# Score tasks issued in pairs during the projections, and a second buffer for the retrieved memory rows, in a fused two-branch attention kernel

## The chip, the cores and the metric

The kernel runs on one core of one Trainium2 chip. A core has a matrix engine (TensorE, PE in the profile; its weight loads are listed apart as PEld), a vector engine (VectorE, DVE), a scalar engine (ScalarE, ACT), a general engine (GpSimd, POOL) and a queue processor (SyncE, SP) that here only issues DMAs. They run side by side, each through its own list of instructions in order, and wait for one another on semaphores. The metric is device time in microseconds (us) of the whole program; lower is better. All inputs and outputs are float32.

## The reference

Two attention branches on the same input of 2048 rows and 512 columns, 32 heads of 16, mixed by a gate per row. Branch A works in four segments of 512 rows: causal softmax attention inside the segment, and beside it a read of a running memory (a 16x16 matrix and a normaliser per head) that earlier segments have filled. Branch B is ordinary full softmax attention.

```python
for s in range(4):                                  # branch A, segment s
    logits = einsum("bhqd,bhkd->bhqk", qs, ks) * scale + mask
    a_dot = einsum("bhqk,bhkd->bhqd", softmax(logits), vs)
    pq = phi(qs)                                    # t + 1 if t > 0 else exp(t)
    num = einsum("bhld,bhde->bhle", pq, M)
    den = einsum("bhld,bhd->bhl", pq, z)[..., None] + 1e-6
    outs.append(g * num / den + (1 - g) * a_dot)
    M = M + einsum("bhld,bhle->bhde", phi(ks), vs)
    z = z + phi(ks).sum(rows)
a = concat(outs) @ wo
b = softmax(qB @ kB.T * scale) @ vB @ wob           # branch B
out = gate * a + (1 - gate) * b
```

## The kernel before

All instructions are issued in the order in which the program writes them; each engine keeps that order.

**Projection stage** (to about 349 us). Queries, keys and values are computed by jobs of 12 matmuls of 128x128 by 128x512 (v_job, L255; qk_job, L274): three products of high and low halves, over four slices of the 512 columns. A job takes one PSUM bank from a pool of six, later four (misc, L95, the bank not used for longest). For a query or key job ScalarE copies the bank into st[:, 0], VectorE subtracts to get the remainder st[:, 1], and SP writes both halves to device memory (two DMAs; st has four buffers). Where branch A needs phi, VectorE takes the minimum with 0 (L285), ScalarE the exponential (L288), VectorE the maximum and sum (L291), all before the bank is free.

The loop of 16 blocks (L722) goes over branch A: block = 4 g + c, for four groups g of eight heads and four segments c. In each block come the query job, the key job, then for c > 0 the memory read: mem_out (L304) multiplies phi(q) by the memory state on TensorE in two halves, ScalarE copies the denominators to recm and the numerators to om, VectorE divides. mem_put (L323), later in the same block, transposes om on TensorE, scales it on ScalarE back into om, and SP writes it out by a DMA (L331). The next memory read, one block later, writes om again; om has one buffer. mem_tr and mem_upd (c < 3) update the memory. Between these parts stand two or three fill jobs of either branch.

**Score tasks for maxima.** The softmax of unit u needs the largest score of each row. s_b (L442) computes a 128x512 block of scores for two heads (two matmuls of 64 rows, in the two halves of the array) into one of two score banks of PSUM (SBK, taken in turn), and VectorE reduces it to maxima (L451, 1.22 us). s_a (L417) does the same with a mask for branch A. A task's matmuls must wait until the reduction of the task before last has freed its bank. From block 4 to block 13 the 38 tasks of units 32 and 0 are spread over the projections: each block adds 3.8 to a quota, and spill (L714), called after each part of a block, issues a task for each whole unit of quota that is there. What is left of them is issued at the end of block 13. In blocks 14 and 15 six tasks of unit 33 follow in the same way, on keys that load_kb(1, ...) brings in.

**From block 14 on** SP's list holds, in order: four DMAs of constant rows (set_aux, L148), load_kb in four parts of four DMAs (L369) with the jobs' and mem_put's writes between them, the writes of block 15's query and key job (L295), and then the four small DMAs of m_rows (L484), which bring the row maxima into the last rows of the query tiles qb and qa. The first score product of the next stage (t_group, L503, tile tb<-qb,kb) reads those rows.

**Score stage** (349 us to the end): 32 rounds, each with one unit of each branch: scores, exponentials on ScalarE, products with the values, and the maxima tasks of the next unit. The last four fill jobs stand in the first round.

Of the kernel before, what the change touches and what calls it, by code (L numbers as in the profile page):

```python
# [7 lines left out]
FT = mybir.dt.float32  # L8
# [10 lines left out]
E = 16  # L19
# [14 lines left out]
def gated_mix_kernel(ctx, tc, x, wq, wk, wv, wo, beta, wqkv, wob, gate_w, out):  # L34
# [36 lines left out]
    X = proj.enter_context(tc.tile_pool(name="proj", bufs=1))  # L71
# [23 lines left out]
    def misc():  # L95
        return bank(mode["misc"])
# [204 lines left out]
    def mem_state(g, c):  # L301
        return MST[c % 2][g % 2]

    def mem_out(g, c):  # L304
        m = mem_state(g, c)[:, :, :E + 1]
        o = X.tile([128, 4, 8, E], FT, name="om")
        r = X.tile([128, 4, 8], FT, name="recm")
        for n in range(2):
            b = misc()[:, :16 * (E + 1)].rearrange("p (i h e) -> p i h e", i=2, h=8)
            for i in range(2):  # L310
                nc.tensor.matmul(b[:, i], PHI[g, 0, c][:, (2 * n + i) * 128:(2 * n + i + 1) * 128], m,
                                 start=True, stop=True)
            nc.scalar.activation(r[:, 2 * n:2 * n + 2], b[:, :, :, E], AF.Copy)
            nc.scalar.activation(o[:, 2 * n:2 * n + 2].rearrange("p i h e -> p (i h) e"),
                                 b[:, :, :, :E].rearrange("p i h e -> p (i h) e"), AF.Copy)
        nc.vector.tensor_scalar(r, r, 1e-6, None, op0=OP.add)
        nc.vector.reciprocal(r, r)
        nc.vector.tensor_tensor(r, r, gate[:, 4 * c:4 * c + 4, None].to_broadcast([128, 4, 8]), op=OP.mult)
        o3 = o.rearrange("p i h e -> p (i h) e")
        nc.vector.tensor_tensor(o3, o3, r.rearrange("p i h -> p (i h)")[:, :, None].to_broadcast([128, 32, E]), op=OP.mult)  # L320
        PHI[g, "o", c] = o
# [258 lines left out]
    def o_cols(c, t):  # L580
        return AT["o"][c % 2][:, :, :, t * 128:(t + 1) * 128]
# [57 lines left out]
    def s_tasks(u):  # L639
        return [todo(s_a, u, *t) for t in ST_A] if u < 32 else [todo(s_b, u, *t) for t in ST_B]  # L640
# [60 lines left out]
    first = s_tasks(32) + s_tasks(0)  # L701
    st33 = [todo(s_b, 33, *t) for t in sorted(ST_B, key=lambda t: t[2])]
    early = st33[:EARLY]
# [8 lines left out]
    quota = 0  # L712

    def spill():  # L714
        nonlocal quota
        if quota >= 1:
            quota -= 1
            (first or early).pop(0)()

    S0 = [b[:, 0] for b in SBK]  # L720
    CUM = (2, 4, 6, 9, 11, 13, 16, 18, 20, 22, 24, 27, 29, 32, 34, 36)
    for blk in range(16):  # L722
# [14 lines left out]
        if c == 3 and g < 3:  # L737
            split_w(0, "A", g + 1, (0,))
        spill()
        if blk == 0:  # L740
            split_wv(3)
            do_beta()
        if blk > 0:
            if pc == 0:
                mem_upd(pg, pc)
        qk_job(0, "A", g, 1, c)
        spill()
        if c == 2 and g < 3:
            load_w("A", g + 1)
# [18 lines left out]
        if c > 0:  # L768
            mt[0] += [todo(mem_out, g, c)]
            mt[2] += [todo(mem_put, g, c)]  # L770
        if c < NC4 - 1:
            mt[1 + (c == 0)] += [todo(mem_tr, g, c)]
        for n in range(3):
            for f in mt[n]:
                f()
            if blk == 14 and n == 2:
                quota = EARLY
            if mt[n]:
                spill()
            if blk == 14:  # L780
                load_kb(1, 1 + n)
            if nf == 35:
                mode["misc"] = [MB, PVB, TB[1]]
            if nf < want:
                fill[nf]()
                spill()
                if nf in (18, 24):
                    load_w("B", 2 + nf // 24)
                if nf in (15, 20, 26):
                    split_w(2 if nf == 20 else 1, "B", nf // 5 - 2)  # L790
                nf += 1
        if blk == 13:
            for f in first:
                f()
            first, quota = [], 0
# [160 lines left out]
    for t in range(4):  # L956
        d = den[:, t * 128:(t + 1) * 128]
        o = o_cols(3, t)[:, 3, 0]
# [36 lines left out]
```

## Time and profile before

| | us |
|---|---|
| median of the runs | 1983.9 |
| lowest, highest of 3 runs | 1976.98, 1985.88 |
| profiled execution, first to last instruction (span) | 1976.0 |
| TensorE busy in the span | 1944.8 |
| VectorE busy | 1630.3 |
| ScalarE busy | 1435.7 |
| GpSimd busy | 257.5 |

The profile records one execution. The span leaves out what lies before the first and after the last instruction; the fastest run lies 0.98 us above it. In the timelines, a row is a run of like instructions on one engine: its start in us from the span's start, its length in us, engine, line of the program, operation, output tile <- input tiles, shapes, and the count. A number in square brackets is the engine's idle time before the row, with what ended it. Lengths of matmuls overlap a little (they are pipelined), so the cost of a piece of work is read from the start of one row to the start of the next. "SPq" rows are DMAs being issued by SP.

### The profile page before, as it was taken

The page shows a single profiled execution, that of the slowest core. Times are in us where ns is not written, and L with a number is a line of the kernel's source. Part 1 is how long each engine was busy: PE and PEld are TensorE (multiplying, and loading weights), DVE is VectorE, ACT ScalarE, POOL GpSimd, SP SyncE. Part 2 cuts the span into 40 slices and gives each one's busy share as a digit, 9 for nine tenths or more (in the row PEclk, how much of TensorE's full clock was granted, in tenths as well). Part 3 has the DMA queues.
Part 4 walks back from the last instruction along what each step waited for, and adds up shares of the span by engine and source line. Part 5 has one row for each costly group of instructions (what it writes and reads, how often), then busy time and mean ns, then how long its engine had stood idle before and what let it go on. Part 6 is the DMA issues. An engine that isn't in the chain of part 4 may idle for free.

```text
span 1976.0 us, 43643 instructions
## 1 busy us (share of the span) xinstructions
PE 1944.8 (98%) x17517; PEld 945.6 (48%) x17517; DVE 1630.3 (83%) x1825; ACT 1435.7 (73%) x2703; POOL 257.5 (13%) x474
## 2 busy tenths in 40 slices
PE   8999999999999999999999999999999999999999
PEld 6887777434344344444444444444444444444435
DVE  6135665899999999999999999999999999999942
ACT  3233332688888888888888888888888888888884
POOL 2200000011210101111010101010101010101012
PEclk9999999999999999999999999999999999999999
DMA  6766656644443444344445353444344444444111
GB/s 205 172 209 183 191 186 173 152 111 114 97 114 88 103 86 103 86 114 86 114 85 112 86 113 86 114 86 114 86 108 91 96 102 87 102 90 103 48 51 57
DMA packets 162742, 222.49 MB, mean 113 GB/s; under 512 B 39260, under 2 KB 89452, under 8 KB 156780
## 3 DMA queue, kind: packets, MB, share of 16 engines
q1 hardware_dynamic: 159596, 211.70, 44.0%
q0 software_dynamic: 2944, 8.00, 2.1%
q8 instruction: 138, 2.26, 0.5%
q14 instruction: 64, 0.52, 0.1%
HBM read 148.21 MB, written 68.16 MB: 109 GB/s over the span
## 4 chain that ended last, share of the span: by engine, by line
PE 90%; DMA 3%; DVE 2%; ACT 2%; issue 1%; SPq 1%; ACTq 0%; DVEq 0%
PE pvb L525 31%; PE tb L503 17%; PE sbk L449 12%; PE mb L503 8%; PE tb L279 3%; PE tb L591 2%; PE mb L279 2%; PE sbk L427 2%; PE pvb L279 2%; PE tb L262 2%; DVE mxb L451 1%; ACT raw L509 1%; PE mb L591 1%; PE mb L262 1%; PE sbk L431 1%
## 5 line engine op out<-in xcount | busy, mean ns | idle before, releaser
L451 DVE TENSOR_REDUCE mxb<-sbk 128x2 f32<-128x1024 f32 x1024 | 1226.1, 1222 | 36.6 <-PE sbk L449 32.4
L509 ACT ACTIVATE raw<-tb 128x512 f32<-128x512 f32 x1557 | 888.2, 598 | 163.1 <-PE tb L503 90.7
L525 PE MATMUL pvb<-raw,vb 128*17 128x256 f32 (+1 forms) x8072 | 639.4, 388 | 0.0
L509 ACT ACTIVATE raw<-mb 128x512 f32<-128x512 f32 x780 | 466.4, 598 | 76.5 <-PE tb L503 44.8
L503 PE MATMUL tb<-qb,xh 64*128 64x512 f32 x872 | 330.8, 496 | 1.7 <-ACT raw L509 1.7
L525 PEld LDWEIGHTS pvb<-raw,vb 128*17 128x17 f32 x8072 | 134.4, 95 | 341.7 <-issue 336.6
L449 PE MATMUL sbk<-xh,qb 64*128 64x512 f32 x1344 | 283.1, 398 | 2.0 <-DMA xh<-dB 0.8
L503 PE MATMUL mb<-qb,xh 64*128 64x512 f32 x445 | 219.6, 494 | 0.0
L503 PEld LDWEIGHTS tb<-qb,xh 64*128 64x128 f32 x872 | 124.4, 183 | 188.1 <-issue 91.4
L512 POOL TENSOR_SCALAR_AFFINE_SELECT raw<-raw 128x256 f32<-128x256 f32 (+1 forms) x320 | 116.1, 363 | 700.1 <-ACT raw L509 692.3
L503 PE MATMUL tb<-qb,kb 64*128 64x512 f32 x471 | 176.3, 496 | 1.4 <-DMA qb<-mr 0.8
L435 DVE TENSOR_REDUCE mx<-sbk 128x2 f32<-128x768 f32 (+1 forms) x128 | 139.8, 1092 | 43.1 <-PE sbk L431 37.1
L449 PE MATMUL sbk<-kb,qb 64*128 64x512 f32 x704 | 150.6, 406 | 1.2 <-DVE mxb L451 1.1
L449 PEld LDWEIGHTS sbk<-xh,qb 64*128 64x128 f32 x1344 | 137.9, 186 | 7.3 <-DVE mxb L451 3.5
L503 PEld LDWEIGHTS mb<-qb,xh 64*128 64x128 f32 x445 | 81.3, 183 | 86.6 <-issue 48.0
L503 PE MATMUL mb<-qb,kb 64*128 64x512 f32 x233 | 115.4, 495 | 0.7 <-DVE st L289 0.7
L565 POOL TENSOR_TENSOR o<-o,d 128x512 f32<-128x512 f32 x31 | 39.8, 1283 | 562.6 <-DMA d<-rd 281.6
L503 PEld LDWEIGHTS tb<-qb,kb 64*128 64x128 f32 x471 | 66.0, 183 | 98.4 <-issue 52.5
L525 PE MATMUL pvb<-raw,va 128*17 128x256 f32 (+2 forms) x1280 | 94.7, 383 | 5.8 <-ACT pvs L534 5.8
L427 PE MATMUL sbk<-ka,qa 64*128 64x256 f32 (+3 forms) x512 | 86.8, 346 | 1.2 <-ACT raw L509 1.2
L503 PE MATMUL tb<-qa,ka 64*128 64x384 f32 (+3 forms) x340 | 79.2, 372 | 0.0
L449 PEld LDWEIGHTS sbk<-kb,qb 64*128 64x128 f32 x704 | 71.6, 185 | 12.6 <-issue 6.5
(273 smaller groups left out, 1790.7 us busy)
## 6 DMA issues: line engine op xcount, KB each, us to landing
xh<-dB SPq DMA_DIRECT2D x38, 512.0 KB
vb<-vdB SPq DMA_DIRECT2D x16, 1088.0 KB
dB<-st SPq DMA_DIRECT2D x64, 256.0 KB
dA<-st SPq DMA_DIRECT2D x64, 256.0 KB
pd<-pvs SPq DMA_DIRECT2D x64, 256.0 KB
kb<-dB SPq DMA_DIRECT2D x22, 512.0 KB
xh<-dB SPq DMA_DIRECT2D x38, 256.0 KB
qb<-dB SPq DMA_DIRECT2D x64, 128.0 KB
```

Of the source, the lines that this page charges most:

```text
L262: nc.tensor.matmul(b, lhs, WV[wi][:, k, :], start=n == 0, stop=n == 11)
L279: nc.tensor.matmul(b, WS[ws][w][wi][:, k, :], (XH, XL)[xi][c][:, k, :], start=n == 0, stop=n == 11)
L427: nc.tensor.matmul(b[:, j, c0:c0 + n], q_of(u)[r, p, i * 128:(i + 1) * 128], k_of(u, p)[r, :n], start=True, stop=False)
L435: nc.vector.tensor_reduce(m[:, :, p, i], b[:, :, :n], axis=AX.X, op=OP.max)
L449: nc.tensor.matmul(b[:, j], q_of(u)[r, p, i * 128:(i + 1) * 128], k_of(u, p)[r, kc * C:(kc + 1) * C], start=True, stop=True)
L451: nc.vector.tensor_reduce(MXB[u][:, :, p, i, kc], b, axis=AX.X, op=OP.max)
L503: nc.tensor.matmul(bs[j][:, c0:c0 + w], k_of(u, h // 2)[r, 128 * it:128 * it + 128], q_of(u)[r, h // 2, q0:], start=True, stop=True)
L509: nc.scalar.activation(pt, bs[j], AF.Exp, scale=SCALE)
L512: nc.gpsimd.affine_select(out=m, in_=m, pattern=[[1, 128]] if n < 2 else [[0, 2], [1, 128]], compare_op=OP.is_ge, fill=0.0, base=0, channe ...
L525: nc.tensor.matmul(PVB[32 * h:32 * h + E + 1, q0 + lo:q0 + hi], vt[:, it, 4 * q + h, :], pt[:, lo:hi], start=it == 0 and lo == 0, stop=it ...
L565: nc.gpsimd.tensor_tensor(o, o, d, op=OP.mult)
L591: nc.tensor.matmul(b, (AT["oh"], AT["ol"])[oi][:, g, a], (AT["wh"], AT["wl"])[wi][:, g, a], start=n == 0, stop=n == 11)
```

## The change

spill waits until two units of quota are there and then issues two tasks in a row; the number of tasks does not change. The tile om gets two buffers (recm beside it keeps one).

```diff
     def mem_out(g, c):
         m = mem_state(g, c)[:, :, :E + 1]
-        o = X.tile([128, 4, 8, E], FT, name="om")
+        o = X.tile([128, 4, 8, E], FT, name="om", bufs=2)
         r = X.tile([128, 4, 8], FT, name="recm")
...
     def spill():
         nonlocal quota
-        if quota >= 1:
-            quota -= 1
-            (first or early).pop(0)()
+        if quota >= 2:
+            quota -= 2
+            for _ in range(2):
+                (first or early).pop(0)()
```

With two units at a time the tasks of a block stand behind its query job and its key job (in blocks 4 and 13 behind the query job alone), no longer behind mem_out and the fill jobs; two masked tasks of unit 0, not one, are left for the end of block 13. In block 14 two pairs follow mem_put and mem_upd, in block 15 one pair follows the query job.

## The prediction

> **What bounds the kernel now.** I read the page first, then the busy time by stretch, then TensorE's waits, then the timelines of TensorE, VectorE and the SP queue around the two edits. The page and the stretch from 200 to 310 us (columns: stretch, length, busy PE, PEld, DVE, ACT, POOL, granted clock, DMA share, GB/s):
>
> ```profile
> PE 1944.8 (98%) x17517; PEld 945.6 (48%) x17517; DVE 1630.3 (83%) x1825; ACT 1435.7 (73%) x2703; POOL 257.5 (13%) x474
> ```
>
> ```profile
> 200.00:310.00 110.00, 110.00 (x549) 82.09 (x548) 73.20 (x108) 36.40 (x78) 3.92 (x6) 1.00 0.60 190
> ```
>
> TensorE has no idle time in the heart of the projection stage; VectorE is busy for two thirds of it. So an edit there is worth what it takes off TensorE's queue, or what it makes TensorE wait. TensorE's waits between 140 and 380 us (total, times, longest) are few:
>
> ```profile
> PE tb L279 <- ACT om L314: 3.0, 1, 3.0
> ...
> PE tb L503 <- DMA qb<-mr: 0.8, 1, 0.8
> ...
> PE pvb L262 <- DVE phi L291: 0.7, 1, 0.7
> ```
>
> The first is the memory rows' single buffer, once, at the end of block 15. TensorE there, with ScalarE and SP (start, length; a number in brackets is idle time before):
>
> ```profile
> 316.99 0.62 PE L311 MATMUL tb<-mst,phi 128*128 128x136 f32 x4
> 317.37 2.12 PE L279 MATMUL tb<-xh,wv 128*128 128x512 f32 x8
> ...
> 338.81 0.49 PE L449 MATMUL sbk<-xh,qb 64*128 64x512 f32 x2
> 342.30 3.78 PE L279 MATMUL tb<-xh,wv 128*128 128x512 f32 x8 [3.00 <-ACT om L314]
> ...
> 347.59 0.92 PE L327 MATMUL mb<-ident,om 128*128 128x128 f32 x4
> 349.33 0.50 PE L503 MATMUL tb<-qb,kb 64*128 64x512 f32 x2 [0.83 <-DMA qb<-mr]
> ```
>
> ```profile
> 341.86 0.38 ACT L314 ACTIVATE om<-tb 128x256 f32<-128x256 f32 x1 [6.65 <-DMA om<-om]
> ```
>
> ```profile
> 311.18 6.96 SPq L148 DMA_DIRECT2D xh<-aux  x4
> ...
> 340.24 3.68 SPq L295 DMA_DIRECT2D dA<-st  x4
> ...
> 344.02 2.58 SPq L484 DMA_DIRECT2D qb<-mr  x2
> ```
>
> ```profile
> 345.34 3.95 DMA qb<-mr
> ```
>
> The reader is to see two things. ScalarE's wait stops TensorE for 3.00 us; but the score stage that follows cannot begin before the rows of m_rows have landed (345.34 + 3.95 = 349.29), and SP issues those in its own time: its queue works from 311.18 to 346.60 with hardly a gap, on transfers ordered before them. The chain of waits goes through both.
>
> **The change, part by part.**
>
> *Doubled buffer.* It removes ScalarE's wait at block 15: the buffer then used was last read by the transfer of block 13, two products back. TensorE would start the last job 3.00 us sooner, and would not run it slowly. How slowly is seen from its rows: 342.30 to 347.59 is 5.29 us, where such a job elsewhere takes 2.88 (below), so 2.4 more, and the four transposes take 347.59 to 348.50, about 0.5 more than the usual 0.4. The granted clock says why:
>
> ```profile
> 344.00:346.00 2.00, 2.00 (x6) 1.52 (x6) 2.00 (x3) 0.00 (x0) 0.00 (x0) 0.50 0.53 184
> ...
> 348.00:350.00 2.00, 1.17 (x10) 0.72 (x8) 0.69 (x1) 1.25 (x3) 0.00 (x0) 0.94 0.32 66
> ```
>
> After 3 us of idling the clock is 0.50, and full again near 348.2, some 5.8 us after work resumed. All this (3.0 + 2.4 + 0.5 = 5.9 us) I cost as a gain of **nothing**: the work that hides it is SP's queue. TensorE would be done with block 15 at about 342.5, then wait for the rows until 349.3, which is late next. If that cover were gone, the gain would be the 5.9 us. What remains is worse than nothing: TensorE now idles some 6.8 us, so it is the score stage that begins at half clock, on the path to the end. 5.8 us at half clock lose 2.9 us of work; the first job alone loses 2.4. I take **+2.6 us**; the lower bound is 0 (the clock returns at once), the upper 2.9 if it returns as it did before.
>
> The Trainium skill ("TensorE: Matmul & The Clock Gate", Part 1) has the clock halve after about 3.4 us without work and return after about 3.4 us of it. By that the loss would be about 1.7 us (an estimate from that page) and the sum 0.9 us lower; the trace agrees on the halving, but its slow stretch was longer.
>
> *Two at a time: what TensorE saves.* Timeline of TensorE, first for a score task alone:
>
> ```profile
> 142.34 2.11 PE L262 MATMUL sbk<-wv,xh 128*128 128x512 f32 x8
> ...
> 145.22 2.03 PE L279 MATMUL tb<-xh,ws 128*128 128x512 f32 x8
> ...
> 184.04 0.63 PE L311 MATMUL pvb<-mst,phi 128*128 128x136 f32 x4
> 184.60 0.49 PE L449 MATMUL sbk<-kb,qb 64*128 64x512 f32 x2
> 185.03 2.13 PE L262 MATMUL tb<-wv,xh 128*128 128x512 f32 x8
> ...
> 188.02 0.49 PE L449 MATMUL sbk<-kb,qb 64*128 64x512 f32 x2
> 188.44 0.65 PE L336 MATMUL tb<-ident,phi 128*128 128x128 f32 x4
> ```
>
> A job of 12 matmuls after another takes 145.22 - 142.34 = 2.88 us; with a task it is 188.44 - 185.03 = 3.41, so a task alone costs 0.53. After mem_out it costs more: the half of the memory product before it takes 0.56 (184.04 to 184.60) against 0.38 without (316.99 to 317.37), the task 0.43, the job after it 2.99 against 2.88: 0.72. A second task behind a first shows only in the score stage:
>
> ```profile
> 372.15 0.64 PE L449 MATMUL sbk<-xh,qb 64*128 64x512 f32 x4
> 372.72 0.63 PE L525 MATMUL pvb<-raw,vb 128*17 128x256 f32 x8
> ...
> 375.21 0.40 PE L449 MATMUL sbk<-xh,qb 64*128 64x512 f32 x2
> 375.54 0.63 PE L525 MATMUL pvb<-raw,vb 128*17 128x256 f32 x8
> ```
>
> Two take 0.57, one 0.33: the second costs 0.24. Of the 38 tasks up to block 13, 19 become second ones; following the quota through the loop, 7 of them come from places after mem_out, 12 from others: 7 x 0.72 + 12 x 0.53 - 19 x 0.24 = **6.8 us saved**.
>
> *Two at a time: what it costs.* Each task needs one of two score banks, and a bank is free when VectorE's reduction of it is done. The rows that time it, TensorE's task after the block's first job, then VectorE's reduction of it:
>
> ```profile
> 213.76 0.51 PE L449 MATMUL sbk<-kb,qb 64*128 64x512 f32 x2
> ...
> 227.20 0.51 PE L449 MATMUL sbk<-kb,qb 64*128 64x512 f32 x2
> ...
> 231.54 0.51 PE L449 MATMUL sbk<-kb,qb 64*128 64x512 f32 x2
> ```
>
> ```profile
> 215.11 1.22 DVE L451 TENSOR_REDUCE mxb<-sbk 128x2 f32<-128x1024 f32 x1
> ...
> 229.91 1.22 DVE L451 TENSOR_REDUCE mxb<-sbk 128x2 f32<-128x1024 f32 x1
> ```
>
> ```profile
> 244.50 0.51 PE L449 MATMUL sbk<-kb,qb 64*128 64x512 f32 x2
> ...
> 260.85 0.51 PE L449 MATMUL sbk<-kb,qb 64*128 64x512 f32 x2
> ```
>
> ```profile
> 247.17 1.22 DVE L451 TENSOR_REDUCE mxb<-sbk 128x2 f32<-128x1024 f32 x1
> 248.30 0.68 DVE L285 TENSOR_SCALAR phi<-tb 128x512 f32<-128x512 f32 x1
> ...
> 264.11 1.22 DVE L451 TENSOR_REDUCE mxb<-sbk 128x2 f32<-128x1024 f32 x1
> ```
>
> Count from the start of a block's first pair. VectorE first has that block's first job to finish, then two reductions 1.13 apart (247.17 to 248.30). In blocks 6 and 10 (c = 2) they end at 3.80 and 4.93. TensorE is back with the second pair at 3.65 (0.24 for the second task, 3.41 for the first and the job); its second task starts at 4.93 and ends at 5.36, not 4.32: 1.1 us of waiting, counted as roundly as the hand-over allows. In 7 and 11 (c = 3) a weight split is queued ahead on VectorE, so the reduction starts at 264.11 - 260.85 = 3.26, the banks come free at 4.39 and 5.52: 1.6 us. In 8 and 12 (c = 0) it starts at 1.35 and both banks are free in time: 0. In 5 and 9 (c = 1) mem_upd gives more time (231.54 - 227.20 + 0.24 = 4.58 against 3.84 and 4.97): 0.2. In block 5 the 0.7 us wait on phi in the table above grows too, since VectorE reaches the second job later: about 0.7 more. Sum 2 x 1.1 + 2 x 1.6 + 2 x 0.2 + 0.7 = **6.5 us**. Behind the waiting task on TensorE stand mem_out and the fill job; ScalarE and VectorE wait for them, but neither is short of time there. Bounds for saving and cost together: -6.8 (no wait) to +6.5 (no saving); I take **-0.3**.
>
> In blocks 14 and 15 the pairs change only when TensorE is done, ahead of the wait for SP: nothing. SP's long run starts from the last job of block 13, so it shifts by the same -0.3.
>
> Sum: -0.3 + 0 + 2.6 = **+2.3 us**. The span of 1976.0 would become 1978.3. The span is 7.9 under the median of the three runs (1983.9) and 0.98 under the fastest; from the median the forecast is **1986.2 us**. The score stage does not give it back: TensorE is as full there as here.
>
> **The rivals.** (1) *Both edits pay in full*: no bank waits (-6.8) and the end of block 15 closes up (-5.9): 1971.2. For it: the wait removed is on the chain of waits. Against: SP's order, and the reductions' times. The Trainium skill ("Trainium Kernel Development and Optimization", Best Practices) would have double-buffering pay like this; SP's row speaks against it here. Chance 0.10. (2) *Pairs pay, the buffer does not*: -6.8 + 2.6 = -4.2, 1979.7. For: VectorE is a third idle. Against: the two banks. Chance 0.14. (3) *Slower*: the clock stays at half beyond the first job of the score stage, through all four left-over fill jobs, since small matmuls and waits stand between them. 4 x 2.4 = 9.6 us, and about half of the 10 us of smaller work up to 371 as well: +14.6, less 0.3, 1998.2. It decides from 356 us on: if the clock is still 0.50 there. For: an idle time twice as long as the one above. Against: the recovery at 348. Chance 0.18. (4) *The change does not act* (another single buffer, recm, holds ScalarE instead): 1983.9; the earlier product's scaling is long over by then. Chance 0.04. My forecast has 0.54.
>
> **How the numbers follow.** About 0.5% (9.9 us) is what a measurement of this kernel can tell from no change. Faster: rival 1, 0.10. Slower: rival 3 and a small part of the forecast, 0.20. Within: 0.70. The forecast's own range, from the runs' spread and the bounds, is 1980 to 1991. The range given, 1977 to 1996, reaches over rival 2 and into rival 3, and leaves out rival 1 and the rest of 3.
>
> **What would show it.** Right: TensorE's wait on om gone, its wait on qb<-mr about 6 us, clock 0.50 behind it, waits of a task on mxb of 1 to 2 us in blocks 6, 7, 10, 11. Wrong: the first score group well before 349 us, no waits on mxb, or an end of block 13 that lies more than 3 us from where it was.

## The result and the profile after

| | before | after |
|---|---|---|
| median of 21 runs, us | 1981.2 | 1984.27 |
| lowest, highest, us | 1976.2, 1986.2 | 1979.7, 1988.8 |
| span of the profiled execution, us | 1976.0 | 1980.9 |

The ratio is 1.0019 with an interval of 1.0011 to 1.0027: about 3.8 us slower (2.2 to 5.3 us, taking the ratio times 1981.2). The forecast was +2.3 us, within 0.5% of before, inside the range given. The page after:

```profile
PE 1943.0 (98%) x17517; PEld 948.6 (48%) x17517; DVE 1627.8 (82%) x1825; ACT 1434.4 (72%) x2703; POOL 256.6 (13%) x474
```

TensorE's waits between 140 and 380 us after (total, times, longest; two smaller ones, 0.8 and 0.5, left out):

```profile
PE sbk L449 <- DVE mxb L451: 5.1, 9, 0.8
PE tb L503 <- DMA qb<-mr: 4.7, 1, 4.7
PE sbk L449 <- DMA xh<-dB: 3.3, 1, 3.3
PE pvb L262 <- DVE phi L291: 1.1, 1, 1.1
```

The wait on om is gone from the list. In its place stand the wait for the rows of m_rows (0.8 before, 4.7 now), a longer wait for the first keys of unit 33 (0.8, now 3.3), and waits of score tasks on the reductions of their banks, which before came to 0.4. Busy TensorE is 1.8 us less than before, yet the span is 4.9 longer. The end of block 15 on TensorE's timeline, after:

```profile
347.01 0.60 PE L327 MATMUL mb<-ident,om 128*128 128x128 f32 x4
352.27 0.50 PE L503 MATMUL tb<-qb,kb 64*128 64x512 f32 x2 [4.65 <-DMA qb<-mr]
...
353.36 3.45 PE L279 MATMUL mb<-xh,wv 128*128 128x512 f32 x8
...
357.66 0.50 PE L503 MATMUL tb<-qb,kb 64*128 64x512 f32 x2
```

Block 15 now closes without the stop on om (a wait of 0.48 us behind VectorE, at 341.3 us, is new), and TensorE idles afterwards. The first fill job of the score stage then takes 357.66 - 353.36 = 4.30 us; before, 2.98 (350.22 to 353.20):

```profile
350.22 2.12 PE L279 MATMUL mb<-xh,wv 128*128 128x512 f32 x8
...
353.20 0.50 PE L503 MATMUL tb<-qb,kb 64*128 64x512 f32 x2
```

The granted clock (third number from the end) says why. After:

```profile
354.00:356.00 2.00, 2.00 (x6) 1.60 (x5) 1.40 (x2) 0.00 (x0) 0.00 (x0) 0.50 0.55 198
356.00:358.00 2.00, 2.00 (x11) 1.34 (x9) 0.00 (x0) 0.23 (x1) 0.00 (x0) 0.93 0.79 227
```

Block 7 after shows the other half of the change, on TensorE's timeline:

```profile
195.96 0.74 PE L449 MATMUL sbk<-kb,qb 64*128 64x512 f32 x4
196.62 2.12 PE L279 MATMUL pvb<-xh,ws 128*128 128x512 f32 x8
...
200.50 0.49 PE L449 MATMUL sbk<-kb,qb 64*128 64x512 f32 x2 [0.83 <-DVE mxb L451]
201.63 0.49 PE L449 MATMUL sbk<-kb,qb 64*128 64x512 f32 x2 [0.64 <-DVE mxb L451]
...
203.31 3.38 PE L279 MATMUL mb<-xh,wv 128*128 128x512 f32 x8
...
207.45 2.02 PE L279 MATMUL pvb<-xh,wv 128*128 128x512 f32 x8
...
260.44 0.74 PE L449 MATMUL sbk<-kb,qb 64*128 64x512 f32 x4
...
267.48 3.67 PE L279 MATMUL tb<-xh,wv 128*128 128x512 f32 x8
...
271.91 2.02 PE L279 MATMUL mb<-xh,wv 128*128 128x512 f32 x8
```

The first pair goes through in 0.66 us (195.96 to 196.62), and both tasks of the second wait for a bank. Behind them and the memory product the next job takes 4.14 us (203.31 to 207.45), not 2.88, and in block 11 its counterpart 4.43 (267.48 to 271.91). There the clock has dropped too, in block 7 as shown and in block 11 to 0.50 from 268 to 270 us:

```profile
202.00:204.00 2.00, 2.00 (x12) 1.86 (x11) 2.00 (x3) 0.75 (x4) 0.00 (x0) 0.67 0.79 246
204.00:206.00 2.00, 2.00 (x6) 1.56 (x5) 1.84 (x6) 0.16 (x1) 0.00 (x0) 0.50 0.61 210
```

To see where the time went, I use three marks on TensorE: the start of the first score task of block 4, the start of mem_upd at the end of block 13, and the first score product. The rows of before, then of after:

```profile
148.09 0.50 PE L449 MATMUL sbk<-kb,qb 64*128 64x512 f32 x2
...
309.64 1.19 PE L350 MATMUL tb<-vm,pk 128*128 128x136 f32 x8
```

```profile
145.74 0.74 PE L449 MATMUL sbk<-kb,qb 64*128 64x512 f32 x4
...
310.73 1.19 PE L350 MATMUL tb<-vm,pk 128*128 128x136 f32 x8
```

| stretch, us | before | after | difference |
|---|---|---|---|
| start to first task | 148.09 | 145.74 | -2.35 |
| first task to the end of block 13 | 161.55 | 164.99 | +3.44 |
| end of block 13 to the first score product | 39.69 | 41.54 | +1.85 |
| first score product to the end | 1626.67 | 1628.63 | +1.96 |
| span | 1976.0 | 1980.9 | +4.9 |

The first line is for the most part not the change's doing: 1.7 us of it are there by 116 us, where a job at 34 us ran at half speed in the one execution and not in the other. The other 0.6 us lies around a short wait behind om in block 2 of before; e1, which has one buffer too, does not lose it. Single executions differ by such amounts, so the differences between kernels below are taken from the ratios, and the marks only say where inside an execution time went. The profiled execution of before is also one of its shorter ones: 1976.98 us, 4.2 below the median, where that of after (1982.58) is 1.7 below.

The last line of the table adds up three things, and only the first goes with the change. From the first row of score products to the next one after the fill job it takes 3.87 us before (349.33 to 353.20) and 5.39 after (352.27 to 357.66): 1.5 us for the half clock. Before has a wait of 1.12 us on a score bank at 443.7 us that after does not have; seven of the twelve traces (before, e1, e3, e5, e7, e9, e10) have one of 0.6 to 1.1 us there. And near 1910 us, behind two waits of 0.34 and 1.17 us that both have, the clock drops in after (0.72 from 1910 to 1915 us) and not in before (1.00), which costs 1.5 us. All twelve traces have the waits of 0.34 and 1.17 us; the drop is in seven of them (after, e1 to e5, e8) and not in before, e6, e7, e9 and e10, so neither of the two follows the pairs or the buffer.

### The profile page after: what moved, and what is told of

Same layout as the page of the kernel before. It is cut to its first block, busy times and chain, and to the rows that moved or that the text cites. A ratio compares the mean times of both kernels' runs of the same rounds, so it can differ in the third digit from the quotient of the medians.

```text
span 1980.9 us, 43644 instructions
## 1 busy us (share of the span) xinstructions
PE 1943.0 (98%) x17517; PEld 948.6 (48%) x17517; DVE 1627.8 (82%) x1825; ACT 1434.4 (72%) x2703; POOL 256.6 (13%) x474
## 4 chain that ended last, share of the span: by engine, by line
PE 90%; DVE 3%; ACT 3%; DMA 2%; issue 1%; SPq 1%; ACTq 0%; DVEq 0%
PE pvb L525 31%; PE tb L503 17%; PE sbk L449 12%; PE mb L503 8%; PE tb L279 3%; PE tb L591 2%; PE mb L279 2%; DVE mxb L451 2%; PE sbk L427 2%; PE tb L262 2%; ACT raw L509 1%; PE mb L591 1%; PE pvb L279 1%; PE sbk L431 1%; PE mb L262 1%
```

## The experiments

After the result I held this theory (A): pairs save work on TensorE but lose it again to waits for score banks, and the second buffer gives nothing because SP's list, on which the rows of m_rows stand, decides when the score stage starts. The rival (B): the whole loss is the second buffer's, through the half clock behind the longer idle time.

**One part alone.** e1_pairs_only takes the second buffer out of the changed kernel; e2_om_only puts it into the kernel before.

```diff
-        o = X.tile([128, 4, 8, E], FT, name="om", bufs=2)
+        o = X.tile([128, 4, 8, E], FT, name="om")
```

> The changed kernel with one om buffer again. Theory A (waits for score banks and the SP queue cost the time, the second buffer gives nothing): TensorE comes to the last job of block 15 late, so little or nothing of the 3.0 us wait on om is left; the time is within 1 us of the changed kernel, about +3.8 us against before. Theory B (the second buffer costs it, through the half clock at the start of the score stage): the loss goes with the buffer, 0 us against before.

Measured: ratio to before 1.0015 (1.0001 to 1.0028), against 1.0019 for both parts together: as A said, and B's 0 lies just outside the interval. TensorE's waits in e1:

```profile
PE sbk L449 <- DVE mxb L451: 5.8, 10, 0.8
PE tb L503 <- DMA qb<-mr: 4.2, 1, 4.2
PE tb L279 <- ACT om L314: 1.2, 1, 1.2
```

The om wait is 1.2, not 3.0: counted from the end of block 13 (308.16 us in e1), TensorE comes there 0.7 us later than before, and the transfer that frees the buffer is done 1.2 us earlier. The wait for the rows is still 4.2, and the first fill job behind it takes 5.15 us (348.97 to 354.12). So the slow start of the score stage comes without the second buffer too.

> The kernel before with two om buffers, tasks one at a time. Theory A: the wait on om is gone, TensorE waits some 6 us for the rows of m_rows instead and starts the score stage at half clock; +1 to +2.5 us against before. Theory B: the whole loss, +3.8 us. Theory C (the buffer pays): -3 to -6 us.

Measured: 1.0002 (0.9991 to 1.0014). This rules out B and C, whose +3.8 us and -3 us lie outside; A's smaller loss lies inside the interval, and so does no loss at all. e2's timeline where the score stage starts:

```profile
348.38 0.79 PE L503 MATMUL tb<-qb,kb 64*128 64x512 f32 x2 [5.49 <-DMA qb<-mr]
...
349.95 3.39 PE L279 MATMUL mb<-xh,wv 128*128 128x512 f32 x8
...
354.21 0.50 PE L503 MATMUL tb<-qb,kb 64*128 64x512 f32 x2
```

The saved wait turned up as 5.49 us in front of the score stage, and the first fill job took 4.26 us. By the run times the slowdown comes with the pairs, though the intervals of e1 and e2 overlap.

**Pairs without the bank waits.** e3_pairs_spaced keeps two tasks in a row but lets at least two calls of spill pass after each pair.

```diff
-        if quota >= 2:
+        gap += 1
+        if quota >= 2 and (gap > 2 or not first):
+            gap = 0
             quota -= 2
```

> The changed kernel, but a pair is followed by at least two calls of spill without a task up to block 13, so a block's second pair stands after its first fill job. Theory A: no waits of a task on mxb in blocks 6, 7, 10, 11, no half clock in 7 and 11, the end of block 13 about 6 us earlier counted from the first pair; the rows of m_rows earlier by 3 to 5 us, time 0 to -2 us against before. Rival: the tasks' order does not matter, +3.8 us as the changed kernel.

Measured: 0.9999 (0.9987 to 1.001), as A said and 1.0019 excluded. The marks in e3:

```profile
148.52 0.74 PE L449 MATMUL sbk<-kb,qb 64*128 64x512 f32 x4
...
304.54 1.19 PE L350 MATMUL tb<-vm,pk 128*128 128x136 f32 x8
...
346.92 0.50 PE L503 MATMUL tb<-qb,kb 64*128 64x512 f32 x2 [4.54 <-DMA qb<-mr]
```

Up to the end of block 13 it takes 156.02 us: 5.5 less than before, 9.0 less than the changed kernel. No task waits on mxb in blocks 4 to 13 and no job there runs slowly. But from there to the first score product it takes 42.38 us, 2.7 more than before, and TensorE waits 4.54 us for the rows, after 4.2 us for the first keys of unit 33 in block 14. The saving is lost in front of the score stage.

**The half clock.** e4_warm adds work that nothing uses to the changed kernel, and e8_om_warm the same (18 matmuls) to the kernel of e2.

```diff
+    for _ in range(14):
+        nc.tensor.matmul(PVB, WS[0][0][0][:, 0, :], XL[0][:, 0, :], start=True, stop=True)
     for k in range(32):
```

> The changed kernel with 14 idle matmuls of 128x512 into PVB between block 15 and the score stage, in TensorE's wait for the rows of m_rows (3.4 us of work that nothing uses). Theory A: granted clock 1.0 behind the wait, the first fill job of the score stage 2.98 us instead of 4.3; -1.5 us against the changed kernel, about +2.3 us against before. Rival (the half clock costs nothing there): no difference to the changed kernel, or slower by up to 3.4 us.

Measured: 1.0007 (0.9995 to 1.0019); the expected +2.3 us is 1.0012. The rows of e4:

```profile
347.69 3.47 PE L907 MATMUL pvb<-xl,ws 128*128 128x512 f32 x14
353.56 0.50 PE L503 MATMUL tb<-qb,kb 64*128 64x512 f32 x2 [2.40 <-DMA qb<-mr]
...
354.45 2.13 PE L279 MATMUL mb<-xh,wv 128*128 128x512 f32 x8
...
357.44 0.50 PE L503 MATMUL tb<-qb,kb 64*128 64x512 f32 x2
```

The job takes 2.99 us again, and from the first row of score products to the next it takes 3.88 us, as before, not 5.39. (The whole stretch to the end is 1626.6 us, as before, too; that is chance, since e4 has the drop near 1910 us and lacks the bank wait at 443.7.)

> The kernel before with two om buffers and 18 idle matmuls of 128x512 (4.4 us of work that nothing uses) in TensorE's wait ahead of the score stage. Theory A (the half clock behind the wait is all that the second buffer costs): clock 1.0, first fill job 2.98 us; about 2.4 us less than with the buffer alone, -2 us against before. Rival: no difference to the buffer alone.

Measured: 0.999 (0.9978 to 1.0002), about -2 us. The rows of e8:

```profile
351.35 0.50 PE L503 MATMUL tb<-qb,kb 64*128 64x512 f32 x2
...
355.23 0.50 PE L503 MATMUL tb<-qb,kb 64*128 64x512 f32 x2
```

3.88 us here as well, where e2 has 5.83 (348.38 to 354.21). Each interval overlaps that of the kernel without the idle matmuls, so the gain in time is likely rather than proved; the shorter job is plain in both traces.

**What sets the start of the score stage.** e5 (the changed kernel), e6 (before with two om buffers) and e7 (e3) issue two of the four parts of load_kb behind m_rows:

```diff
-            if blk == 14:
-                load_kb(1, 1 + n)
+            if blk == 14 and n == 0:
+                load_kb(1, 1)
...
             m_rows(0)
+            load_kb(1, 2)
+            load_kb(1, 3)
```

> The changed kernel with the third and fourth part of load_kb(1, ...) issued behind m_rows, not ahead of it. Theory A (SP's list sets the start of the score stage): the rows of m_rows land some 6.6 us earlier, before TensorE is done with block 15; its wait on them is gone, the clock stays at 1.0; -4.7 and -2.0 us, so about -3 us against before. Rival (the transfers, not SP's list, hold the rows back): the wait stays near 4.7 us and the time at +3.8.

Measured: 0.9998 (0.9988 to 1.0008), 4 us better than the changed kernel's ratio, but the expected -3 us against before lies outside. In e5 the wait for the rows has gone; a wait of 0.41 us on a bank is what is left there:

```profile
348.42 0.60 PE L327 MATMUL mb<-ident,om 128*128 128x128 f32 x4
349.14 0.49 PE L503 MATMUL tb<-qb,kb 64*128 64x512 f32 x1
350.04 0.49 PE L503 MATMUL tb<-qb,kb 64*128 64x512 f32 x1 [0.41 <-DVE st L289]
```

From the end of block 13 (310.75) to the first score product it takes 38.39 us, 3.15 less than in the changed kernel; the slow jobs of blocks 7 and 11 are still there, and so are 3.5 us of waiting for the first keys of unit 33.

> The kernel before with two om buffers and the same later load_kb parts, tasks one at a time. Theory A: here the second buffer pays, since nothing holds TensorE at the start of the score stage; about -5.7 us of waiting and -2.5 us of half clock against the kernel with the buffer alone, -7 us against before. Rival: about 0.

Measured: 0.998 (0.9969 to 0.999), -4 us. The buffer does pay here, by less than expected (-7 us lies outside the interval): a wait of 2.4 us for the rows and a slow first job remain.

> The changed kernel with pairs spaced as in e3 and the later load_kb parts. Theory A: the 5.5 us that spaced pairs save up to block 13 reach the end in part, as far as SP lets the first tasks of unit 33 begin; wait on the rows of m_rows under 1 us, clock 1.0; -6 to -9 us against before. Rival: as e3, 0.

Measured: 0.9971 (0.9959 to 0.9983), -5.7 us, a version faster than both kernels. Its waits:

```profile
PE sbk L449 <- DMA xh<-dB: 5.9, 1, 5.9
...
PE tb L503 <- DMA qb<-mr: 0.6, 1, 0.6
```

TensorE is now held for 5.9 us in block 14, by the first keys of unit 33. The last two runs aim at that, by moving four DMAs of constant rows from SP to GpSimd: e10 in the kernel of e2, e9 in that of e7.

```diff
-                set_aux(KB[1][:, p], 0, nc.sync)
+                set_aux(KB[1][:, p], 0)
```

> The kernel before with two om buffers and the four constant-row DMAs of block 14 issued by GpSimd; load_kb in its old place. Theory A: SP reaches m_rows some 6 to 7 us earlier, the wait on its rows is gone and the clock stays at 1.0 at the start of the score stage; -6 to -8 us against before. Rival: as the buffer alone, 0.

Measured: 1.0001 (0.9987 to 1.0014): a miss. SP's list in e10:

```profile
313.16 10.48 SPq L369 DMA_DIRECT2D xh<-dB  x4
...
345.41 2.84 SPq L484 DMA_DIRECT2D qb<-mr  x2
```

SP no longer spends 7 us on the four DMAs, but the next four take 10.48 us, where they took 4.01 before, and m_rows comes hardly earlier: 34.6 us after the end of block 13 (310.81), in e2 35.5, before 34.4. Giving part of the list to another queue, with the same transfers, did not make it shorter here; putting transfers behind m_rows did help.

> As e7 (spaced pairs, two om buffers, later load_kb parts), and the four constant-row DMAs of block 14 issued by GpSimd, so that SP's list is some 7 us shorter ahead of the first keys of unit 33. Theory A: TensorE's wait on those keys (5.9 us in e7) falls under 1 us, nothing waits on the rows of m_rows; about 5 us less than e7, -10 to -12 us against before. Rival (the keys wait for their own transfer, not for SP's list): as e7, -5.7 us.

Measured: 0.9964 (0.9948 to 0.998), -7.1 us, the fastest of all; its interval overlaps that of e7, and the wait for the keys is still 5.3 us, so the expected mechanism is not there. What the first keys wait for, transfer time or the list's backlog, stays open.

## Why the prediction was right, step by step

**The doubled buffer: nothing gained, then a slow start.** Right in kind. SP's list was the cover that it named: the om wait went and the wait for the rows rose to 4.7 us in the changed kernel and 5.5 in e2. The forecast was 6 us, and 2.6 us of loss by the half clock. Measured, from the first row of score products to the next: 1.5 us more than before in the changed kernel, 2.0 in e2, 2.9 in e1, 0 in e4 and e8. So the 2.6 was mis-sized by 1.1 us for this kernel, inside its own bounds of 0 to 2.9. In the run times, e2's loss is not clear of zero. One reading was loose: the transposes' 0.91 us is a length and the usual 0.4 a time from start to start; length against length (0.92 against 0.60 in the row at 347.01) they cost 0.3 more, not 0.5. Only rival 1 used that.

**What pairs save: 6.8 us.** Right. e3 gains 5.5 us up to block 13, while two of its waits between 140 and 310 us are longer or new:

```profile
PE pvb L262 <- DVE phi L291: 1.4, 1, 1.4
PE tb L311 <- DVE mst L355: 0.5, 1, 0.5
```

The first was 0.7 before, the second did not exist; 5.5 + 0.7 + 0.5 = 6.7.

**What pairs lose to banks: 6.5 us.** Right in place and close in size, but something was missing. TensorE's waits in blocks 6, 7, 10 and 11 are 0.94, 1.47, 0.86 and 1.47 us. The changed kernel loses 3.44 us from the first task to the end of block 13, where the step had -0.3; that is beyond the 3 us that the prediction named as a sign of being wrong, if one counts from the first task (1.1 us from the start of the span). Of that, the two slow jobs of blocks 7 and 11 make 4.14 + 4.43 - 2 x 2.88 = 2.8 us. The remaining 0.6, with the 6.8 saved, puts the bank waits at 7.4 us, 0.9 over the step. The prediction took the half clock for a matter of long idle times only, and did not ask it of the bank waits. e1 has one such slow job and loses 1.95 us, e3 has none.

**SP shifts with the end of block 13.** This step fell. It had SP's long run begin with the last job of block 13. SP's list after:

```profile
306.08 5.62 SPq L295 DMA_DIRECT2D dB<-st  x4
311.81 1.04 SPq L331 DMA_DIRECT2D om<-om  x1
312.94 2.31 SPq L295 DMA_DIRECT2D dB<-st  x2
315.35 6.97 SPq L148 DMA_DIRECT2D xh<-aux  x4
```

SP is still writing earlier results when block 13 ends at 310.73, and starts its long run 4.6 us after that mark; before, 1.5 us after it (311.18 against 309.64). This alone would not show it, since the distance varies between executions: 4.5 us in e5, 3.0 in e4 and 2.2 in e1, with pairs as in the changed kernel, and 2.0 to 3.8 us in e2, e6 and e8, with single tasks. e3 shows it:

```profile
310.32 6.22 SPq L148 DMA_DIRECT2D xh<-aux  x4
...
342.30 2.38 SPq L484 DMA_DIRECT2D qb<-mr  x2
```

Block 13 ends at 304.54 there, 5.1 us earlier than before, but the long run begins at 310.32, 0.9 us earlier, and m_rows comes 37.8 us after the mark, in the kernel before 34.4. e7 is like it (304.49 and 312.10). So an earlier end of block 13 does not bring SP's list forward by as much: SP is held by its own backlog there, and time won on TensorE in blocks 4 to 13 mostly ends in front of it. That is also why e3, without bank waits, is no faster than before.

**The sum.** +2.3 forecast, about 3.8 measured (2.2 to 5.3). (The forecast of 1986.2 us stood on the median of three runs, 1983.9; the median of 21 is 1981.2.) That the total came so near is in part luck. The prediction had nearly nothing from the pairs (-0.3) and the whole loss from the buffer (+2.6); alone, the pairs measured +3.0 us (e1, 0.2 to 5.5) and the buffer +0.4 (e2, -1.8 to 2.8). In the two traces the three stretches behind the first task come to +7.25 us, 4.95 over the forecast: 2.8 for the slow jobs in blocks 7 and 11, 0.9 for the bank waits, 1.85 for the stretch in front of the score stage, less 0.6 in the last one. The run times put the whole change at 3.8, so these traces overstate it, and how the 3.8 us divide among the steps stays open. **The rivals:** the first two (-12.7 and -4.2 us) needed the pairs to go without bank waits, and these came; e3, which has none, shows that SP's list would have kept the gain back even then. The third, a clock that stays at half through four fill jobs, did not come: it was 0.93 from 356 to 358 us. The fourth fell with the vanished om wait.

## What to carry to other kernels

Before a wait is taken off a busy engine, look for the next thing that the same point needs, and on whose queue that stands: here a gain of 5.9 us was already promised to a DMA in a list that was late. Grouping small tasks saved their switching cost (6.7 us in e3), and gave it back in waits where two groups followed each other faster than the other engine emptied the two banks; a gap between the groups, as in e3, avoids that. For a queue that is behind, ordering urgent small transfers ahead of bulk ones helped here (e5 to e7), and handing four transfers to a second queue did not (e10).

## What the runs showed of the hardware beyond that

- Two short waits with a single task between them, 0.83 and 0.64 us, were followed by a fall of the granted clock from 1.00 to 0.50 in block 7. The Trainium skill ("TensorE: Matmul & The Clock Gate", Part 1) names idle windows of about 3.4 us; these waits are shorter than that. It is not the same in each execution: of the other three traces with those waits, e5 shows the slow job in blocks 7 and 11, e1 in block 11 alone and e4 in block 7 alone. The waits of blocks 6 and 10 (0.30 or 0.23 and 0.64 us) are followed by no slow job in any of the four. The drop near 1910 us, in seven of twelve traces, is the same kind of thing, behind 0.34 and 1.17 us.
- Slow stretches ended after 3 to 6 us of work: about 5.8 us in the kernel before, 4 us at the start of the score stage after.
- A two-matmul task of 64 rows between jobs of 128 rows costs TensorE 0.53 us, behind another such task 0.24.
